# Attention on TensorE: from single heads in high and low parts to pairs of native float32 heads on the halves of the array

## The chip, the cores and the metric

One core of a Trainium2 chip runs one launch. The metric is the device time of the launch in microseconds. The kernel before takes 884.78 us (median of 3 runs, 884.65 to 886.75).

## What is computed

Attention with a causal window of 128 and a distance bias (batch 4, 8 heads, 576 positions, head dimension 64), then two feed-forward networks on the 2,304 x 512 result. From the reference:

```python
scores = scale * np.matmul(q, k.transpose(0, 1, 3, 2))
slopes = 2.0 ** (-8.0 * (np.arange(H, dtype=np.float32) + 1) / H)
bias = slopes[:, None, None] * (-np.abs(rel).astype(np.float32))[None, :, :]
mask = (rel >= 0) & (rel < window)
scores = np.where(mask, scores + bias[None], -1000000000.0)
...
attn = np.exp(scores)
attn = attn / (np.sum(attn, axis=-1, keepdims=True) + 1e-09)
return np.matmul(attn, v).astype(np.float32)
...
a = x @ w1
b = x @ w2
h = a * b @ w3
return (h @ w_out).astype(np.float32)
...
h = np.maximum(x @ w_in, 0.0)
return (h * h @ w_out).astype(np.float32)
```

The slope of head h is 2^-(h+1).

## The kernel before

**The whole.** The weights come as 64-bit words and are made into float32 on the chip (`conv_g`, `conv_s`, `conv_m`: two passes of VectorE over every weight tile on L307, two more on any engine). The product W3·W_out is formed first, native float32, on L733 (`p_w34`, 64 matmuls of 512 columns). Then, for each batch and each half of its 576 positions, `p_ab` multiplies x with W1 and W2 and `p_y` the product with W3·W_out; results go to DRAM as y. The second network follows with seven products in place of eight per 2x2 block (`p_r`, `p_o`). All large products but W3·W_out are float32 in two rounded parts: `mm3` (L165 to L168) sends high x high, high x low and low x high, one pass each.

**Attention.** A head has five blocks of 128 queries (the last one of 64 new queries), each against at most 256 keys. `p_qk` writes the scores of blocks 0 and 1, of 2 and 3 and of 4 into three PSUM tiles "s", of which there are two buffers, each one bank. `l_min` (L438, VectorE) adds the bias, reduces and stores the negated scores in "e" (block 4 in "p4"), `l_exp` (L446, ScalarE) takes the exponential, `l_sum` and `l_norm` divide. `p_tr1` and `p_tr2` transpose P on TensorE into PSUM tiles "t" (nine transposes of 128x128, L489 to L501; one uses a swapped identity, `swap`), `l_pth` copies them to SBUF, `p_pva` and `p_pvb` multiply with V, and `l_eva`, `l_evb`, `l_ad*` bring the result into `xf`. For each pair of heads `t_xh` and `t_xl` split `xf` into the high and low part of x, in tiles of half a batch's positions.

**Two kinds of head.** Heads 0 to 8 (`NQ`, `NV`, L16, L17) are native: q, k, V and P stay float32; the scores have 64 rows of contraction (`64*128` in the records), P·V has 64 output columns (`128*64`, its last piece `64*64`). k is first multiplied by 2^(h+1) (`t_kn`), so that one bias table `bm` serves all heads. TensorE records two matmuls and two weight loads for each native matmul. Heads 9 to 31 are split into high and low parts: q is stacked as high over low on 128 rows and met with k high and k low (L468, L469); V is laid side by side as high and low, and P high and P low are both sent through it (L528 to L532, L552), so that the partial results have to be added afterwards (L585, L590, L603).

**What sets the order.** `Plan` is given each step with a rank, engines and a cost, the steps it waits for and the buffers that it takes and gives back; `run()` then simulates the engines, picks among the steps that can start within 0.1 us the one of the lowest rank, and the instructions are recorded in that order for every engine. Heads have rank -13.66 + 10 n, the matmuls of the networks 1000 and more, so that heads go first where their data is ready. Each engine executes its own list in that order.

Of the kernel before, what the change touches and what calls it, by code (L numbers as in the profile page):

```python
# [15 lines left out]
NQ = frozenset(range(9))  # L16
NV = frozenset(range(9))  # L17
# [6 lines left out]
HALF = S // 2  # L24
WIN = 128


class Plan:
# [24 lines left out]
    def run(self):  # L53
# [15 lines left out]
        while ready:  # L69
            cands = []  # L70
            for n in ready:
# [3 lines left out]
                for h in takes:  # L75
                    p = pool[self.holds[h][0]]
                    if len(p) <= keep:
                        ok = False
                        break
                    t0 = max(t0, min(p))  # L80
# [44 lines left out]
def fused_kernel(  # L125
# [62 lines left out]
    swap = const.tile([128, 128], F32, name="swap")  # L188
    nc.gpsimd.memset(swap, 0.0)
    for base in (64, -64):  # L190
        nc.gpsimd.affine_select(
            out=swap, in_=swap, pattern=[[-1, 128]], compare_op=ALU.not_equal,
            fill=1.0, base=base, channel_multiplier=1,
        )
    bm = const.tile([128, 2 * WIN], F32, name="bm")
    nc.gpsimd.iota(
        bm, pattern=[[8, 2 * WIN]], base=-8 * WIN, channel_multiplier=-8,
# [3 lines left out]
        out=bm, in_=bm, pattern=[[-1, 2 * WIN]], compare_op=ALU.is_ge,  # L201
# [3 lines left out]
        out=bm, in_=bm, pattern=[[1, 2 * WIN]], compare_op=ALU.is_gt,  # L205
        fill=-1.0e30, base=0, channel_multiplier=-1,
    )

# [37 lines left out]
    def w_dma(kb, n=1):  # L246
# [4 lines left out]
            u=10, u34=4, wo=4, qkraw=1, qk=2, vraw0=1, vraw1=1, vs=2, e=2, p40=1, p41=1, s=2, t=1,  # L251
            pt1=1, pt2=1, a=1, b=1, xf=1, ta=1, tb=1, g=3, asb=2, gf=2, gt=8, ye=2,
            yA=14, yB=6, s0=1, t2a=1, t2b=1, v6=6, st=2, c1=2, U2=1, U4=1, U3=1, C=4, X=5, fo=4, fq=5, ww=4,
            **{f"x0_{k}": 1 for k in range(6)}, **{f"x1_{k}": 1 for k in range(8)},
# [82 lines left out]
    QS = [(i * 128, min(128, S - i * 128)) for i in range(5)]  # L337
    vraw = [at.tile([128, 5, D], F32, tag=f"vraw{i}", name=f"vraw{i}") for i in range(2)]
    for t in vraw:
        nc.gpsimd.memset(t[64:128, 4, :], 0.0)  # L340

    p4 = [at.tile([128, 256], F32, tag=f"p4{i}", name=f"p4{i}") for i in range(2)]
    for t in p4:
        nc.gpsimd.memset(t, 0.0)
    pts = {}


    def new_pt(nat):
        dt = F32 if nat else F32R
        t = at.tile([128, 1 if nat else 2, 1280], dt, tag="pt", name="pt")  # L350
        z = t[:, :, 512:768]
        nc.gpsimd.memset(z if dt == F32 else f(z), 0.0)
        pts[nat] = t

    HD = [dict() for _ in range(B * H)]
    xt = {}

    def t_load_qk(n):
        b, h = divmod(n, H)
        d = HD[n]  # L360
        if n in NQ:
            d["qs"] = at.tile([64, S], F32, tag="qs", bufs=2, name="qn")
            d["kh"] = at.tile([64, S], F32, tag="kh", bufs=2, name="kn")
            nc.sync.dma_start(out=d["qs"], in_=qk[b, h, 0])
            nc.sync.dma_start(out=d["kh"], in_=qk[b, h, 1])
        else:
            d["raw"] = at.tile([128, 2, S], F32, tag="qkraw", bufs=1, name="qkraw")
            for r in range(2):
                nc.sync.dma_start(out=d["raw"][64 * r:64 * r + 64], in_=qk[b, h].rearrange("t d s -> d t s"))

    def t_load_v(n):
        b, h = divmod(n, H)
        if n in NV:
            vd = HD[n]["vs"] = at.tile([128, 5, D], F32, tag="vs", bufs=2, name="vn")
        else:
            vd = vraw[n % 2]
        nc.sync.dma_start(out=vd[:, 0:4, :], in_=v_main[b, h].rearrange("p (c d) -> p c d", d=D))
        nc.sync.dma_start(out=vd[0:64, 4, :], in_=v_rest[b, h])

    def slope(n):  # L380
        return float(2 ** (n % H + 1))

    def t_kn(n, e):
        k = HD[n]["kh"]
        scaled(e, k, k, slope(n))

    def t_qh(n, e):
        d = HD[n]
        d["qs"] = at.tile([128, S], F32R, tag="qs", bufs=2, name="qs")
        copy(e, d["qs"], d["raw"][:, 0])  # L390

    def t_kh(n, e):
        d = HD[n]
        d["kh"] = at.tile([128, S], F32R, tag="kh", bufs=2, name="kh")
        nc.scalar.activation(out=d["kh"], in_=d["raw"][:, 1], func=ACTF.Copy, scale=slope(n))

    def t_ql(n, e):
        d = HD[n]
        sub(ENG[e], d["qs"][64:128], d["raw"][64:128, 0], f(d["qs"][64:128]))

    def t_kl(n, e):
        d = HD[n]
        d["kl"] = at.tile([128, S], F32R, tag="kl", bufs=2, name="kl")
        nc.vector.scalar_tensor_tensor(
            out=d["kl"], in0=d["raw"][:, 1], scalar=slope(n), in1=f(d["kh"]), op0=ALU.mult, op1=ALU.subtract
        )

    def t_vh(n, e):
        d = HD[n]
        vs = d["vs"] = at.tile([128, 5, 2 * D], F32R, tag="vs", bufs=2, name="vs")  # L410
        hi = (n % 2) * D
        copy(e, vs[:, :, hi:hi + D], vraw[n % 2])

    def t_vl(n, e):
        vs = HD[n]["vs"]
        hi = (n % 2) * D
        lo = D - hi
        sub(ENG[e], vs[:, :, lo:lo + D], vraw[n % 2], f(vs[:, :, hi:hi + D]))

    def part_of(n, i):  # L420
        if i == 4:
            return p4[n % 2][64:128, 0:192]
# [910 lines left out]
```

## Time and profile before

| | |
|---|---|
| time, median of 3 runs | 884.78 us |
| the single runs | 886.75, 884.65, 884.78 us |
| profiled execution, span from first to last instruction | 882.3 us |
| median of the runs less that span | 2.5 us |
| TensorE busy, matmuls | 868.4 us |
| VectorE, ScalarE, GpSimd busy | 680.2, 520.9, 191.9 us |
| HBM read, written | 90.67, 36.70 MB |

For the profiled execution the span alone is given; the fourth line shows what lies around it against the median run. Busy time of a matmul contains its tail in the array, so the length of a block of matmuls is read from start to start. In the rows, PE is TensorE's matmuls, PEld its weight loads, DVE VectorE, ACT ScalarE, POOL GpSimd; `64*128` means rows and columns of the array in use.

### The profile page before, as it was taken

To read this page: it belongs to the slowest core of one execution; us is meant where nothing else is said; L and a number is where in the kernel's file an instruction comes from. 1 tells how busy PE (TensorE), PEld (TensorE's weight loads), DVE (VectorE), ACT (ScalarE), POOL (GpSimd) and SP (SyncE) were. 2 spreads that over 40 slices of the span, in tenths; PEclk is the share of its full clock that TensorE was granted. 3 is DMA by queue.
4 is the path that set the end of the run, shared out by engine and by line. 5 is a ranking of instruction groups with operands and counts; after the bars stand their busy time and mean duration, and the time that the engine had idled before them with its cause. 6 is when DMAs were issued, how large, how long until landed. Compare 5 with 4: busy or idle time off the path is not lost.

```text
span 882.3 us, 16171 instructions
## 1 busy us (share of the span) xinstructions
PE 868.4 (98%) x5888; PEld 805.9 (91%) x5888; DVE 680.2 (77%) x1372; ACT 520.9 (59%) x1062; POOL 191.9 (22%) x234
## 2 busy tenths in 40 slices
PE   7999999999999999999999999999999899999998
PEld 4544459999999999999999999999999899999998
DVE  4878878888798897878676858775678888888772
ACT  5778766666767666667423446543566676556540
POOL 4212113222302312211010337351156200000000
PEclk7999999999999999999999999999999899999999
DMA  6787222441435334342477145453476564444310
GB/s 210 289 289 231 104 81 82 136 146 48 137 84 167 106 106 129 106 131 71 143 245 258 56 166 181 168 180 108 153 245 208 153 182 124 143 139 136 99 53 30
DMA packets 90703, 128.42 MB, mean 146 GB/s; under 512 B 8832, under 2 KB 70784, under 8 KB 88576
## 3 DMA queue, kind: packets, MB, share of 16 engines
q1 hardware_dynamic: 90624, 127.40, 45.7%
q8 instruction: 46, 0.75, 0.4%
q14 instruction: 33, 0.27, 0.1%
HBM read 90.67 MB, written 36.70 MB: 144 GB/s over the span
## 4 chain that ended last, share of the span: by engine, by line
PE 95%; DVE 2%; DMA 1%; issue 1%; ACT 1%; POOL 0%; SPq 0%; DVEq 0%; ACTq 0%; POOLq 0%
PE X L168 13%; PE X L166 13%; PE X L167 13%; PE g L166 11%; PE g L167 11%; PE g L168 11%; PE g L733 7%; PE s L466 2%; PE a L523 2%; PE t L489 2%; PE s L469 2%; PE s L468 1%; PE a L532 1%; PE b L552 1%; DMA m_scro<-u 1%; PE a L528 1%
## 5 line engine op out<-in xcount | busy, mean ns | idle before, releaser
L166 PE MATMUL g<-x,wu 128*128 128x288 f32 x512 | 154.1, 301 | 1.6 <-ACT a_sb L171 1.0
L167 PE MATMUL g<-x,wu 128*128 128x288 f32 x512 | 151.7, 296 | 0.0
L168 PE MATMUL g<-x,wu 128*128 128x288 f32 x512 | 151.1, 295 | 0.0
L166 PEld LDWEIGHTS g<-x,wu 128*128 128x128 f32 x512 | 96.4, 188 | 2.4 <-ACT a_sb L171 1.3
L167 PEld LDWEIGHTS g<-x,wu 128*128 128x128 f32 x512 | 96.8, 189 | 0.3 <-issue 0.3
L168 PEld LDWEIGHTS g<-x,wu 128*128 128x128 f32 x512 | 96.5, 188 | 0.0
L1119 ACT ACTIVATE C<-C 128x384 f32<-128x384 f32 x96 | 47.8, 521 | 64.8 <-issue 35.2
L166 PE MATMUL g<-gt,wu 128*128 128x288 f32 x256 | 76.5, 299 | 0.0
L167 PE MATMUL g<-gt,wu 128*128 128x288 f32 x256 | 75.7, 296 | 0.0
L168 PE MATMUL g<-gt,wu 128*128 128x288 f32 x256 | 75.4, 295 | 0.0
L213 POOL TENSOR_SCALAR e<-e,st 128x256 f32<-128x256 f32 (+1 forms) x59 | 29.3, 507 | 200.9 <-DVE st L456 136.8
L1093 DVE TENSOR_TENSOR C<-X,U 128x384 f32<-128x384 f32 (+1 forms) x99 | 51.2, 520 | 24.3 <-PE X L168 21.1
L446 ACT ACTIVATE e<-e,st 128x256 f32<-128x256 f32 (+1 forms) x128 | 60.5, 474 | 14.8 <-DVE st L438 14.2
L167 PE MATMUL X<-yA,u 128*128 128x384 f32 x192 | 65.0, 339 | 0.0
L166 PE MATMUL X<-yA,u 128*128 128x384 f32 x192 | 65.0, 339 | 0.0
L168 PE MATMUL X<-yA,u 128*128 128x384 f32 x192 | 65.0, 339 | 0.0
L733 PE MATMUL g<-raw 128*128 128x512 f32 x128 | 63.4, 625 | 0.0
L171 ACT ACTIVATE ww<-fq 128x1024 fp32r<-128x1024 f32 x35 | 37.0, 1059 | 42.4 <-PE X L168 24.1
L171 ACT ACTIVATE pt<-t 128x512 fp32r<-128x512 f32 (+1 forms) x64 | 38.3, 598 | 34.5 <-PE t L501 17.8
L167 PE MATMUL X<-u,ww 128*128 128x256 f32 x198 | 55.6, 281 | 0.0
L166 PE MATMUL X<-u,ww 128*128 128x256 f32 x198 | 55.5, 280 | 0.0
L168 PE MATMUL X<-u,ww 128*128 128x256 f32 x198 | 55.5, 280 | 0.0
(218 smaller groups left out, 2649.1 us busy)
## 6 DMA issues: line engine op xcount, KB each, us to landing
s_scr<-C SPq DMA_DIRECT2D x96, 192.0 KB, 2.0
u<-in_w2io_dram SPq DMA_DIRECT2D x32, 512.0 KB, 4.5
qkraw<-in_qk_dram SPq DMA_DIRECT2D x46, 288.0 KB, 4.2
fo<-s_scr SPq DMA_DIRECT2D x20, 512.0 KB, 4.1
raw<-in_w3t_dram SPq DMA_DIRECT2D x8, 1024.0 KB, 6.6
raw<-in_w_dram SPq DMA_DIRECT2D x8, 1024.0 KB, 6.1
fq<-s_scr SPq DMA_DIRECT2D x16, 512.0 KB, 4.1
y_scr<-ye SPq DMA_DIRECT2D x32, 144.0 KB, 1.8
```

The costliest lines, as they stand in the source:

```text
L166: nc.tensor.matmul(o, wh, xh, start=start, stop=False)
L167: nc.tensor.matmul(o, wh, xl, start=False, stop=False)
L168: nc.tensor.matmul(o, wl, xh, start=False, stop=stop)
L171: nc.scalar.activation(out=o, in_=i, func=ACTF.Copy)
L213: nc.gpsimd.tensor_scalar(out=o, in0=i, scalar1=c, scalar2=1.0, op0=ALU.mult, op1=ALU.mult)
L446: nc.scalar.activation(out=e, in_=e, func=ACTF.Exp, bias=st[:, 0, i:i + 1], scale=-1.0, accum_out=st[:, 1, i:i + 1],)
L466: nc.tensor.matmul(o, qb, d["kh"][:, k0:k1], start=True, stop=True)
L469: nc.tensor.matmul(o, qb, d["kl"][:, k0:k1], start=False, stop=True)
L489: nc.tensor.transpose(t[:, 128 * c:128 * c + 128], src, ident)
L733: nc.tensor.matmul(gw[fi], wl, wr, start=c == 0, stop=c == 7)
L1093: nc.vector.tensor_tensor(out=t_(o, tag), in0=bank[g, P], in1=cs[g, i], op=ALU.add)
L1119: nc.scalar.activation(out=x, in_=x, func=ACTF.Relu)
```

## The change

Two neighbouring heads are handled as a pair, all 32 heads native. q and k of the pair lie in one tile, the first head on partitions 0 to 63, the second on 64 to 127, and `p_qk` sends a matmul of the first head and one of the second in turn; each head writes its own score tile, so that a group of scores takes both buffers of "s". `p_pv` does the same with P·V: the first head fills PSUM partitions 0 to 63, the second 64 to 127 of one bank. `bm` is now a table per head, made by seven scalings of the first; k is no longer multiplied. All transposes use the plain identity. x is split straight from PSUM (`t_xh`, `t_xl`), into tiles of a whole batch's positions for which there are seven slots (`NX`), where there were six and eight of half the length. The planner now counts how many buffers of a kind a step takes. Ranks: -13.66 + 20 m for pair m; the other ranks stay.

```diff
+NE = 3
+NX = 7
...
+    bm = at.tile([128, H, 2 * WIN], F32, name="bm")
+    b0 = bm[:, 0]
     nc.gpsimd.iota(
...
+    for h in range(1, H):
+        nc.vector.tensor_scalar(out=bm[:, h], in0=b0, scalar1=0.5 ** h, scalar2=None, op0=ALU.mult)
...
+        if n % 2 == 0:
+            PR[n // 2]["qk"] = at.tile([128, 2, S], F32, tag="qk", bufs=2, name="qk")
+        r = 64 * (n % 2)
+        nc.sync.dma_start(out=PR[n // 2]["qk"][r:r + 64], in_=qk[b, h].rearrange("t d s -> d t s"))
...
         nc.vector.tensor_tensor_reduce(
             out=part_of(n, i), in0=ps, in1=bmi, op0=ALU.add, op1=ALU.min,
+            scale=-0.125, scalar=3.0e38, accum_out=stat[n % 4][rows(i), 0, i:i + 1],
         )
...
+    def p_qk(m, g):
+        t = PR[m]["qk"]
+        for r in range(2):
+            HD[2 * m + r].setdefault("s", []).append(ps_s.tile([128, 512], F32, tag="s", name="s"))
+        for i in ((0, 1), (2, 3), (4,))[g]:
+            q0 = min(128 * i, S - 128)
+            k0 = max(0, (i - 1) * 128)
+            w = min(S, (i + 1) * 128) - k0
+            o = 256 * (i % 2)
+            for r in range(2):
+                h = slice(64 * r, 64 * r + 64)
+                nc.tensor.matmul(
+                    HD[2 * m + r]["s"][g][:, o:o + w], t[h, 0, q0:q0 + 128], t[h, 1, k0:k0 + w],
+                    start=True, stop=True,
+                )
+
...
+    def l_pt(n, g, e):
+        if g == 0:
+            HD[n]["pt"] = at.tile([128, 1024], F32, tag="pt", bufs=NE, name="pt")
+        copy(e, HD[n]["pt"][:, 512 * g:512 * g + 512], HD[n]["t", g])
+
+    PV = (
+        ((0, 0, 0, 256), (1, 128, 256, 256), (2, 256, 512, 128)),
+        ((3, 0, 768, 192), (2, 0, 640, 128), (4, 128, 960, 64)),
+    )
+
+    def p_pv(m, g):
+        o = PR[m][g] = ps_v.tile([128, 512], F32, tag="ab"[g], name="ab"[g])
+        for x, (kb, c, src, w) in enumerate(PV[g]):
+            for r in range(2):
...
+                    o[64 * r:64 * r + 64, c:c + w], vt[m % 2][:, r, kb, :], HD[2 * m + r]["pt"][:, src:src + w],
+                    start=x == 0, stop=x == 2, skip_group_check=True,
...
+    def x_slot(m):
+        return m % NX
+
+    def t_xh(m, g, e):
+        b, p = divmod(m, H // 2)
+        if g == 0:
+            k = x_slot(m)
+            xt[b, p] = (xg if k < 4 else xb[0]).tile([128, 2, S], F32R, tag=f"x_{k}", name="x")
+        c0, c1 = XC[g]
+        copy(e, xt[b, p][:, 0, c0:c1], PR[m][g][:, 0:c1 - c0])
+
+    def t_xl(m, g):
+        b, p = divmod(m, H // 2)
+        c0, c1 = XC[g]
+        sub(nc.vector, xt[b, p][:, 1, c0:c1], PR[m][g][:, 0:c1 - c0], f(xt[b, p][:, 0, c0:c1]))
...
+        for g, w in enumerate((448, 512, 192)):
+            add(f"qk{g}_{m}", r + 1, {"pe": w_nat(w) + 0.1}, lambda e, g=g: p_qk(m, g), [f"ldq{n}" for n in heads] + last,
+                [f"s{g}_{n}" for n in heads], [f"qk{m}"])
+            last = [f"qk{g}_{m}"]
...
+        for g, w in enumerate((640, 384)):
+            add(f"pv{g}_{m}", r + 8, {"pe": w_nat(w) + 0.1}, lambda e, g=g: p_pv(m, g),
+                [f"pt{x}_{n}" for x in range(2) for n in heads] + [f"ldv{m}"], [f"{'ab'[g]}{m}"],
+                [f"v{m}"] + [f"pt_{n}" for n in heads])
+        k = x_slot(m)
+        hold(f"x{b}{p}", f"x_{k}", 4 * NF1)
+        for g, w in enumerate((QA, S - QA)):
+            add(f"xh{g}_{m}", r + 9, w_copy(w, True), lambda e, g=g: t_xh(m, g, e),
+                [f"pv{g}_{m}"] + ([f"xh0_{m}"] if g else ["gp"] if k >= 4 else []), [] if g else [f"x{b}{p}"], [f"{'ab'[g]}{m}"])
+            add(f"xl{g}_{m}", r + 9, w_tt(w, "d"), lambda e, g=g: t_xl(m, g), [f"xh{g}_{m}"], [], [f"{'ab'[g]}{m}"])
...
+    for m in range(B * H // 2):
+        add_pair(m, RANK["h0"] + 20.0 * m)
```

In the order of instructions this shows on TensorE. The names: s, t, a, b and g are PSUM tiles (scores, transposes, P·V, products), kh, kl, qs, qk, kn, qn hold q and k, pt is P transposed, v and vs are V, x and wu operands of the first network. First the stretch with the products of the first network, between two of its chains, before:

```order
L168 MATMUL g<-x_886,wu 128x288
L528 MATMUL a<-pt,vs 128x512
L529 MATMUL a<-pt,vs 128x256
L532 MATMUL a<-pt,vs 128x256 x4
L552 MATMUL b<-pt,vs 128x192 x4
L468 MATMUL s<-kh,qs 128x192
L469 MATMUL s<-kl,qs 128x192
L166 MATMUL g<-x_340,wu 128x288
```

and now, between two such chains:

```order
L169 MATMUL g<-x,wu 128x288
L448 MATMUL a<-pt,v_127 64x256 x4
L448 MATMUL a<-pt,v_127 64x128 x2
L448 MATMUL b<-pt,v_127 64x192 x2
L448 MATMUL b<-pt,v_127 64x128 x2
L448 MATMUL b<-pt,v_127 64x64 x2
L167 MATMUL g<-x,wu 128x288
```

P·V of one head, ten single-pass matmuls on the whole array and followed at once by the next head's scores, has become twelve native matmuls that go in turn to the first and the second head of a pair; the scores stand elsewhere, group by group. Second, the beginning, where W3·W_out (g<-raw) is formed, before:

```order
L466 MATMUL s<-kn,qn 128x192
L523 MATMUL a<-pt,vn 64x512
L523 MATMUL a<-pt,vn 64x256 x2
L545 MATMUL b<-pt,vn 64x192
L546 MATMUL b<-pt,vn 64x64
L466 MATMUL s<-kn,qn 128x192
L466 MATMUL s<-kn,qn 128x256 x3
L733 MATMUL g<-raw 128x512 x2
```

and now:

```order
L542 MATMUL g<-raw 128x512
L416 MATMUL s<-qk 128x256 x4
L448 MATMUL a<-pt,v_127 64x256 x4
L448 MATMUL a<-pt,v_127 64x128 x2
L448 MATMUL b<-pt,v_127 64x192 x2
L448 MATMUL b<-pt,v_127 64x128 x2
L448 MATMUL b<-pt,v_127 64x64 x2
L542 MATMUL g<-raw 128x512 x3
L416 MATMUL s<-qk 128x192 x2
L416 MATMUL s<-qk 128x128 x2
L416 MATMUL s<-qk 128x256 x2
```

Where P·V and scores of one head stood together, a group of scores of a later pair, P·V of a whole pair and pieces of W3·W_out now follow each other. Counted over the whole list, TensorE has 44 separate blocks of scores (`L416`) and 16 of P·V (`L448`) with 51 returns to matmuls of the whole array; before there were 16 blocks of native scores, 9 of native P·V and 21 returns. Up to the last matmul of W3·W_out the new list has the scores of five pairs and P·V of four, the old one all of heads 0 to 8 and the scores of head 9.

## Rows read from the trace of the kernel before

**Rows 1.** The page, busy time of each engine, its share of the span, instructions.

```profile
PE 868.4 (98%) x5888; PEld 805.9 (91%) x5888; DVE 680.2 (77%) x1372; ACT 520.9 (59%) x1062; POOL 191.9 (22%) x234
```

**Rows 2.** Stretches: busy us of PE, PEld, DVE, ACT, POOL; clock; DMA share; GB/s.

```profile
20.00:128.00 108.00, 107.31 (x365) 53.93 (x364) 88.39 (x189) 81.63 (x173) 20.86 (x27) 1.00 0.59 203
128.00:440.00 312.00, 311.38 (x2404) 309.36 (x2403) 257.96 (x692) 205.13 (x524) 67.96 (x92) 1.00 0.39 112
```

**Rows 3.** The page, the chain that ended last, by engine.

```profile
PE 95%; DVE 2%; DMA 1%; issue 1%; ACT 1%; POOL 0%; SPq 0%; DVEq 0%; ACTq 0%; POOLq 0%
```

**Rows 4.** Waits of TensorE: who, for whom, us in total, times, longest.

```profile
PE t L622 <- POOL bm L204: 3.4, 1, 3.4
PE X L168 <- DVE st L174: 2.2, 1, 2.2
```

**Rows 5.** Timeline of TensorE, native heads: start, us, instruction, shapes, count.

```profile
23.60 0.33 PE L497 MATMUL t<-swap,p 128*128 128x128 f32 x1
23.77 0.27 PE L498 MATMUL t<-ident,p 128*128 128x128 f32 x1
...
23.98 0.27 PE L500 MATMUL t<-ident,e 128*128 128x128 f32 x1
24.09 0.27 PE L501 MATMUL t<-ident,e 128*128 128x128 f32 x1
24.30 0.59 PE L466 MATMUL s<-kn,qn 64*128 64x192 f32 x2
24.81 1.94 PE L523 MATMUL a<-pt,vn 128*64 128x512 f32 x6
26.59 0.49 PE L545 MATMUL b<-pt,vn 128*64 128x192 f32 x2
27.00 0.33 PE L546 MATMUL b<-pt,vn 64*64 64x64 f32 x2
27.26 1.89 PE L466 MATMUL s<-kn,qn 64*128 64x192 f32 x8
29.07 2.08 PE L733 MATMUL g<-raw 128*128 128x512 f32 x4
31.08 0.59 PE L466 MATMUL s<-kn,qn 64*128 64x192 f32 x2
31.60 0.66 PE L489 MATMUL t<-ident,e 128*128 128x128 f32 x4
```

**Rows 6.** The same for a head in high and low parts.

```profile
181.34 0.25 PE L468 MATMUL s<-kh,qs 128*128 128x192 f32 x1
...
182.28 0.29 PE L166 MATMUL g<-x,wu 128*128 128x288 f32 x1
...
185.95 0.33 PE L468 MATMUL s<-kh,qs 128*128 128x192 f32 x1
...
186.24 0.32 PE L166 MATMUL g<-x,wu 128*128 128x288 f32 x1
...
189.46 0.40 PE L528 MATMUL a<-pt,vs 128*128 128x512 f32 x1
...
190.72 0.60 PE L489 MATMUL t<-ident,e 128*128 128x128 f32 x4
```

**Rows 7.** Groups by line and shape: busy us, mean ns of one, idle before.

```profile
L733 PE MATMUL g<-raw 128*128 128x512 f32 x128 | 63.4, 625 | 0.0
...
L307 DVE SCALAR_TENSOR_TENSOR raw<-raw 128x1024 uint32<-128x1024 uint32 x40 | 50.0, 1257 | 3.9 <-issue 1.8 <-POOL p L213 1.3
...
L438 DVE CUSTOM_DVE_ANT_0 e<-s,bm 128x256 f32<-128x256 f32 x96 | 37.1, 418 | 0.6 <-PE s L469 0.4
...
L174 DVE TENSOR_TENSOR pt<-t,pt 128x512 fp32r<-128x512 f32 x46 | 31.6, 688 | 5.7 <-ACT pt L171 4.5
...
L404 DVE SCALAR_TENSOR_TENSOR kl<-qkraw,kh 128x576 fp32r<-128x576 f32 x23 | 19.0, 824 | 1.9 <-ACT kh L395 1.7
...
L603 DVE TENSOR_TENSOR xf<-a,ta 64x512 f32<-64x512 f32 x23 | 15.8, 686 | 0.9 <-POOL ta L590 0.4
```

More of the change, by code (lines that the diff above doesn't have):

```diff
@@ L186, in fused_kernel @@
     make_identity(nc, ident)
[L188 to L195, printed above, removed]
+    bm = at.tile([128, H, 2 * WIN], F32, name="bm")
+    b0 = bm[:, 0]
     nc.gpsimd.iota(
-        bm, pattern=[[8, 2 * WIN]], base=-8 * WIN, channel_multiplier=-8,
+        b0, pattern=[[4, 2 * WIN]], base=-4 * WIN, channel_multiplier=-4,
         allow_small_or_imprecise_dtypes=True,
@@ L334, in add_weights @@
         add("cl" + k, rank, w_tt(1024), lambda e: conv_lo(key, e), ["ch" + k], [], ["raw" + k])
[L337 to L342, printed above, removed]
+    QA = 384
+    vt = [at.tile([128, 2, 5, D], F32, tag=f"v{i}", name=f"v{i}") for i in range(2)]
+    for t in vt:
+        nc.gpsimd.memset(t[64:128, :, 4, :], 0.0)
+    p4 = [at.tile([128, 256], F32, tag=f"p4{i}", name=f"p4{i}") for i in range(4)]
     for t in p4:
         nc.gpsimd.memset(t, 0.0)
[L345 to L353, printed above, removed]
+    stat = [at.tile([128, 3, 5], F32, tag=f"st{i}", name=f"st{i}") for i in range(4)]
+    for t in stat:
+        nc.gpsimd.memset(t, 1.0)
     HD = [dict() for _ in range(B * H)]
+    PR = [dict() for _ in range(B * H // 2)]
     xt = {}
@@ L359, in t_load_qk @@
         b, h = divmod(n, H)
[L360 to L385, printed above, removed]
@@ L444, in l_exp @@
         e = part_of(n, i)
-        st = HD[n]["st"][128 - QS[i][1]:128]
+        st = stat[n % 4][rows(i)]
         nc.scalar.activation(
@@ new lines, in p_tr @@
+    def p_tr(n, g):
+        e, q = HD[n]["e"], p4[n % 4]
+        t = HD[n]["t", g] = ps_t.tile([128, 512], F32, tag="t", name="t")
+        if g == 0:
+            todo = ((0, e[:, 0, 128:256]), (128, e[:, 1, 0:128]), (256, e[:, 1, 128:256]), (384, e[:, 2, 0:128]))
+        else:
+            todo = (
+                (384, q[:, 128:256]), (320, q[:, 0:128]), (256, e[:, 3, 128:256]),
+                (0, e[:, 2, 128:256]), (128, e[:, 3, 0:128]),
+            )
+        for c, src in todo:
+            nc.tensor.transpose(t[:, c:c + 128], src, ident)
@@ L537, in p_pvb @@
-    def p_pvb(n):
-        d = HD[n]
-        vs = d["vs"]
-        pt = pts[n in NV]
-        o = ps_v.tile([128, 512], F32, tag="b", name="b")
-        d["b"] = o
-        if n in NV:
-            o = o[(n % 2) * 64:(n % 2) * 64 + 64]
-            nc.tensor.matmul(o[:, 0:192], vs[:, 3, :], pt[:, 0, 1088:1280], start=True, stop=False)
-            nc.tensor.matmul(
-                o[:, 128:192], vs[0:64, 4, :], pt[0:64, 0, 768:832], start=False, stop=True
-            )
-            return
-        for kb, c in ((3, 1088), (4, 640)):
-            for part in range(2):
-                nc.tensor.matmul(
-                    o[:, 0:192], vs[:, kb, :], pt[:, part, c:c + 192],
-                    start=(kb == 3 and part == 0), stop=(kb == 4 and part == 1),
-                )
```

337 lines of the change are left out of this document (71 added, 266 removed).

## The prediction

> **What bounds the kernel now.** I read the busy shares first: TensorE is busy for 98% of the span, VectorE for 77%, ScalarE for 59% [rows 1]. The table by stages shows three stretches of interest: a start of 20 us, then 20 to 128 us (the products W3·W_out and the first nine heads), then 128 to 440 us (the other 23 heads between the products of the first network). In the second TensorE is busy for 107.31 of 108 us, in the third for 311.38 of 312 [rows 2], always at the full clock. The chain that ended last is TensorE for 95% of its length [rows 3], and the waits of TensorE that the trace can name are one of 3.4 us at the start and some of 2.2 us and less [rows 4]. So the time is the length of TensorE's own stream: what VectorE, ScalarE and the DMA queues are spared is worth nothing by itself, and each column that TensorE streams, each weight load that stands open and each pause between matmuls counts.
>
> What the attention costs on TensorE is read from the starts of its blocks. A native head (0 to 8): the eight records of its first four score blocks (960 columns, two passes each) run from 27.26 to 29.07 us, the last block (192 columns) from 31.08 to 31.60, P·V from 24.81 to 27.26 [rows 5]: 1.81 + 0.52 + 2.45 = 4.78 us. A head in high and low parts (9 to 31): scores 181.34 to 182.28 and 185.95 to 186.24, P·V 189.46 to 190.72 [rows 6]: 0.94 + 0.29 + 1.26 = 2.49 us. The two score blocks of the native head differ by 768 columns and 1.29 us: **1.68 ns for a column of a native matmul**, 0.84 ns in each pass. What is left of the 0.52 us after 192 columns is 0.20 us, which does not grow with the columns: the first weights are loaded in the open, and the array empties before it changes its division. The same shows elsewhere: the last transpose before a block of halves takes 0.21 us from start to start (24.09 to 24.30) where its neighbour takes 0.11, and the first one behind such a block 0.17 (23.60 to 23.77) [rows 5]. So a full-array stretch between two blocks pays 0.16 us. P·V pays 0.06 at its start (1.78 us for 1,024 columns, that is 1.72) and 0.09 behind its 192 columns (0.41 for 0.32): 0.15.
>
> Before, then: 9 x 4.78 + 23 x 2.49 + 21 returns to the full array x 0.16 = 43.0 + 57.3 + 3.4 = **103.7 us**.
>
> **The change on TensorE.** A head now has 1,088 score columns (128 + 3 x 256 + 192) and 1,024 in P·V, all native: 2,112 x 1.68 = 3.55 us. All 32 heads: 113.5 us if the two halves of the array take turns. The order shows 44 blocks of scores and 16 of P·V with 51 returns to the full array, as each group of scores needs both score banks and so stands alone between other work: 44 x 0.20 + 16 x 0.15 + 51 x 0.16 = 19.4 us. The trace before never has two matmuls on different halves next to each other, so the overlap of the halves is not shown and is bounded. Upper end, no overlap: 113.5 + 19.4 = 132.9, **29.2 us more**. Lower end, full overlap: 56.8 + 19.4 = 76.2, 27.5 us less.
>
> I take a value between, from the order of the passes. A matmul is two passes, and the program gives first head, second head, first head and so on. A pass must follow the pass before it on its own half and cannot start ahead of the pass before it in the stream. So the second pass of the first head runs beside the first pass of the second, and the next pair joins on; only the first and the last pass of a block are alone. Two matmuls of 256 columns on each half take 5 x 0.215 = 1.08 us where eight passes in turn take 1.72; the group of 128 and 256 also 1.08, since a pass of 128 columns (0.107) is no longer than the load of its weights (0.20 less the 0.09 of the emptying, 0.11); the group of 192 takes 3 x 0.161 = 0.49; P·V, with six matmuls a half, 2.00 instead of 3.44. Together 4.65 us a pair, 16 x 4.65 + 19.4 = 93.8, **9.9 us less** than before. I choose this over no overlap because of the row nearest to it: the array pauses when the division changes, even between two P·V matmuls of one head (26.59 to 27.00, from 128*64 to 64*64), and not between matmuls of one division [rows 5]; the hardware does hold the halves as units. If the halves' weight loads run beside each other too, the group of 128 and 256 columns takes 0.86 instead of 1.08, 3.5 us less in all; that is the low end of the forecast. The Trainium skill, "TensorEngine Tiling (Array Packing)", Key Properties, says that different tiles load weights and multiply in parallel; by that rule the sum would be 13.4 us less than before, and no run here shows it.
>
> **How much of it arrives.** Of the 103.7 us, 47.6 lie ahead of 128 us: the nine native heads with their returns and the scores of the tenth head. The new order has there, up to the last product of W3·W_out, the scores of five pairs and P·V of four: 5 x 2.65 + 4 x 2.00 + 11 blocks x 0.20 + 4 x 0.15 + 14 returns x 0.16 = 26.3 us, so TensorE has 21 us less to do. From 128 us on it has 11 more: a pair costs 5.9 us with its pauses, two heads in parts 4.98. In the earlier stretch VectorE is busy for 88.39 of 108 us [rows 2], of it 40 passes of 1,257 ns over the weight words [rows 7], which stay as they are. VectorE's list up to the last weights for W3·W_out, at the durations of the trace, adds up to 83 us, about 5 less than before. From 128 to 440 us VectorE is busy for 257.96 of 312 us, 0.83 [rows 2]. At that share 83 us take 100, while TensorE would be through after 87. So between 0 and 13 us of the 21 do not come; I take 4, as TensorE can draw heads forward.
>
> Nothing else is on the path. VectorE loses the low parts of P (46 x 688 ns), of K (23 x 824), the sums into x (23 x 686), 66 us in all [rows 7], and shorter pieces beside them. The third stretch is covered by TensorE, which stands idle there for 0.62 us by the records [rows 2]; so this is worth 0, and I allow 3 us for waits too short to show as idle. The seven new table scalings, 256 columns each, are put at no more than a reduction of 256 columns (0.42 us [rows 7]), 3 us at the start, under the first scores; the table is built without the swap matrix ahead of it, which can only shorten the 3.4 us [rows 4]. The late heads' q and k were loaded twice each and are now loaded once, covered. The new wait, scores of a group until VectorE has read both banks (four reductions of 0.42 us [rows 7], 1.7 us), has behind it on TensorE the products of the network, which the order puts in between: 24 of them between the last two groups of a pair; eight shorter ones take 0.94 us [rows 6], so these take 2.8 us or more. A pair that waits for its slot of x has the second products of the batch as cover.
>
> Sum: 882.3 - 9.9 + 4 = 876.4 us of span. The median of the runs shown is 884.78, 2.5 above the span of the profiled execution: **878.9 us**.
>
> **The rivals.**
> 1. The halves do not overlap, and the change doesn't do what it says: 884.8 + 29.2 = 914. For it: no record before shows overlap, and native matmuls run pass after pass. Against it: the pauses at each new division. It decides as soon as a second head's first pass starts after the end of the first head's second. This is the other side.
> 2. Weights are loaded ahead by one matmul alone, so the second half's first pass starts 0.11 us (scores) or 0.06 us (P·V) behind the pass beside it, and the next ones slip: scores 3.18 a pair instead of 2.65, P·V 2.38 instead of 2.00; 16 x 0.9 = 14 more, 893. For it: no row shows a load that runs ahead of two matmuls, and 0.20 us stand open at every block. With P·V alone so, 16 x 0.38 = 6 more: 885. For that form speaks the Trainium skill, "TensorE: Matmul & The Clock Gate", What overlaps and what doesn't: weight loads overlap running matmuls only when their row groups differ; the two halves of P·V share their rows. No row here decides it.
> 3. The stretch up to 128 us is handed to VectorE and the weight words: 13 to all of the 21 us do not come, 884.8 - 9.9 + 17 = 892. For it: the share of 0.83, and ScalarE at 81.63 of 108 us [rows 2]. Against it: W3·W_out is 63.4 us of TensorE [rows 7] and stands between the heads in small pieces. It decides when the last weights for W3·W_out are ready later than about 112 us.
>
> **How the numbers follow.** Forecast 0.50 (its own range 868 to 888: with parallel loads and nothing lost 871, with 13 lost 888, and 3 beyond the low end for VectorE's relief), no overlap 0.25, loads one ahead in both 0.07, in P·V alone 0.08, VectorE as the bound 0.10. A difference of 0.3%, 2.7 us, is about what a measurement of this kernel can tell. Faster: 0.42 of the forecast and 0.01 of the rest, 0.43. Same: 0.05 of the forecast, 0.05 of P·V alone, 0.02 of the third, 0.12. Slower: 0.03 + 0.25 + 0.07 + 0.02 + 0.08 = 0.45. The range 868 to 915 takes in the case of no overlap and the low end.
>
> **What would show it.** In the trace after: a group of scores with 256 columns takes about 1.1 us plus 0.2 from start to the next work, not 1.7 plus 0.2; P·V about 2.15 us, not 3.6. W3·W_out ends some 16 us sooner than at 128 us. From there to the end of the attention TensorE stays above 99%, with about 0.9 us more for a pair than two heads had. Scores of 1.9 us a group would make the prediction wrong by the first rival; a TensorE that stands idle before 110 us, by the third.

## The result, and the profile after the change

The changed kernel takes **864.76 us** (median of four runs, 864.54 to 865.28), the kernel before 884.71 beside it (884.32 to 886.75): a ratio of 0.977, 95% interval 0.9758 to 0.9782. The forecast was 878.9 with a range from 868 to 915. The direction was right, the size was not: the change brings 20 us, more than three times the 5.9 foreseen, and the time lies below the range. The profiled execution took 865.28 us, its span is 863.4.

TensorE is still the bound. The page's line that answers to [rows 1]:

```profile
PE 846.0 (98%) x5952; PEld 774.7 (90%) x5952; DVE 565.3 (65%) x1146; ACT 449.2 (52%) x932; POOL 159.3 (18%) x199
```

The stretches that answer to [rows 2] (busy us of PE, PEld, DVE, ACT, POOL; granted clock; DMA share; GB/s):

```profile
20.00:128.00 108.00, 104.13 (x495) 58.84 (x494) 88.43 (x180) 74.36 (x165) 27.19 (x31) 0.96 0.58 194
128.00:440.00 312.00, 312.00 (x2460) 291.95 (x2461) 177.26 (x508) 158.34 (x435) 42.25 (x66) 1.00 0.40 127
```

Two things are new. VectorE falls from 0.83 to 0.57 of the third stretch. And TensorE, which had 0.69 us without work between 20 and 128 us, now has 3.87, at a mean clock of 0.96.

Where the time comes from is seen in single blocks. The timeline of TensorE for a group of scores with 256 columns, two matmuls of each head (start, us from the first start to the last end, instruction, count):

```profile
200.45 0.60 PE L432 MATMUL t<-ident,e 128*128 128x128 f32 x4
200.98 1.13 PE L416 MATMUL s<-qk 64*128 64x256 f32 x8
202.04 0.40 PE L167 MATMUL g<-x,wu 128*128 128x288 f32 x1
```

The next work starts 1.06 us after the group. That is 0.86 us for eight passes, and the 0.20 us that [rows 5] gave for a block's open load and emptying; the forecast said 1.08 and 0.20. The same view cut to the first hundredth of a microsecond of this block, and the instructions of the line there (durations in ns, smallest, median, largest):

```profile
200.98 0.49 PE L416 MATMUL s<-qk 64*128 64x256 f32 x2
```

```profile
L416 PEld LDWEIGHTS s<-qk x2: 182/182/183, 201.0 to 201.0; 64*128 64x128 f32 x2
L416 PE MATMUL s<-qk x2: 480/480/480, 201.0 to 201.0; 64*128 64x256 f32 x2
```

Two passes and two weight loads are under way at once: each pass is recorded with 0.48 us, and both lie within 0.49. By the single records the first pass of the second head starts 6 ns after the first pass of the first head, and so on for all four pairs of passes, 0.215 us apart. The second head does not wait for the first head's second pass. P·V, and the score group with 128 columns behind it:

```profile
209.88 1.30 PE L448 MATMUL a<-pt,v 128*64 128x256 f32 x12
211.02 0.83 PE L448 MATMUL b<-pt,v 128*64 128x192 f32 x12
211.77 0.93 PE L416 MATMUL s<-qk 64*128 64x128 f32 x8
212.63 0.40 PE L167 MATMUL g<-gt,wu 128*128 128x288 f32 x1
```

P·V of a pair takes 1.89 us (forecast 2.15 with its pauses), the group of 128 and 256 columns 0.86 (forecast 1.28 with them).

TensorE's time, counted from the start of one pass to the start of the next, with idle time apart; the warm-up matmuls at the very start, 3.6 us before and 3.7 after, are left out:

| us | before | after | difference |
|---|---|---|---|
| scores | 51.4 | 44.5 | -6.9 |
| P·V | 52.5 | 30.6 | -21.9 |
| transposes, with the returns to the full array | 30.3 | 32.8 | +2.5 |
| W3·W_out | 59.8 | 60.7 | +0.9 |
| all other products, with returns | 670.5 | 673.6 | +3.0 |
| idle | 7.6 | 11.2 | +3.6 |

The last product of W3·W_out in the timelines (start, us), before and after:

```profile
128.22 0.61 PE L733 MATMUL g<-raw 128*128 128x512 f32 x1
```

```profile
111.42 0.61 PE L542 MATMUL g<-raw 128*128 128x512 f32 x1
```

It ends at 112.0 us (before: 128.8), 16.8 sooner. From there to TensorE's last product it is 747.9 us, 2.5 less than before. The added idle time is in the first 112 us (7.8 us, in the kernel before 2.0 up to the same product); the waits of TensorE there (who, for whom, us in total, times, longest), which answer to [rows 4]:

```profile
PE t L432 <- ACT pt L172: 3.9, 5, 0.8
PE t L474 <- POOL bm L199: 2.7, 1, 2.7
PE s L416 <- DMA qk<-in_qk_dram: 1.9, 2, 1.2
PE s L416 <- DVE st L383: 1.8, 3, 0.9
PE g L542 <- DVE raw L303: 0.3, 1, 0.3
```

The second of these is the wait ahead of TensorE's first matmul, which the 7.8 us do not count.

### The profile page after: what moved, and what is told of

The parts are those of the page before. It is cut to its first block, busy times and chain, and to the rows that moved or that the text cites. A ratio compares the mean times of both kernels' runs of the same rounds, so it can differ in the third digit from the quotient of the medians.

```text
span 863.4 us, 15706 instructions
## 1 busy us (share of the span) xinstructions
PE 846.0 (98%) x5952; PEld 774.7 (90%) x5952; DVE 565.3 (65%) x1146; ACT 449.2 (52%) x932; POOL 159.3 (18%) x199
## 4 chain that ended last, share of the span: by engine, by line
PE 96%; DVE 1%; DMA 1%; SPq 0%; ACT 0%; issue 0%; DVEq 0%
PE X L169 14%; PE X L168 14%; PE X L167 14%; PE g L167 13%; PE g L169 12%; PE g L168 12%; PE g L542 7%; PE s L416 4%; PE t L432 4%; PE a L448 2%; PE b L448 1%; DMA qk<-in_qk_dram 1%; ACT pt L172 0%; DVE fq L980 0%; SPq L353 0%
## 5 line engine op out<-in xcount | busy, mean ns | idle before, releaser
L595 DVE TENSOR_TENSOR gf<-g,a_sb 128x288 f32<-128x288 f32 x64 | 29.2, 457 | 103.3 <-PE g L169 100.3
L172 ACT ACTIVATE a_sb<-g 128x288 f32<-128x288 f32 x64 | 26.2, 410 | 92.0 <-PE g L169 91.9
L902 DVE TENSOR_TENSOR C<-X,U 128x384 f32<-128x384 f32 (+1 forms) x99 | 51.1, 520 | 26.7 <-PE X L169 21.0
L383 DVE CUSTOM_DVE_ANT_0 e<-s,bm 128x256 f32<-128x256 f32 (+1 forms) x128 | 43.8, 386 | 32.2 <-PE t L432 15.7
L210 POOL TENSOR_SCALAR e<-e,st 128x256 f32<-128x256 f32 (+1 forms) x58 | 29.3, 519 | 152.3 <-DVE st L399 83.8
L167 PE MATMUL X<-u,ww 128*128 128x256 f32 x198 | 55.5, 280 | 0.0
```

What stands on the lines that cost most here:

```text
L167: nc.tensor.matmul(o, wh, xh, start=start, stop=False)
L172: nc.scalar.activation(out=o, in_=i, func=ACTF.Copy)
L210: nc.gpsimd.tensor_scalar(out=o, in0=i, scalar1=c, scalar2=1.0, op0=ALU.mult, op1=ALU.mult)
L383: nc.vector.tensor_tensor_reduce(out=part_of(n, i), in0=ps, in1=bmi, op0=ALU.add, op1=ALU.min, scale=-0.125, scalar=3.0e38, accum_out=stat ...
L902: nc.vector.tensor_tensor(out=t_(o, tag), in0=bank[g, P], in1=cs[g, i], op=ALU.add)
```

## The experiments

Two questions: do the halves really run beside each other, and what sets how far one may run ahead? And what took back some 9 us of a gain that, with full overlap, would have been 27.5? The theory drawn from the trace: each half works through a list of its own; and in the start the gain meets waits and half clock. The rivals stand in each expectation.

**Both heads' scores on one half.** In the scores of the odd heads

```
-                h = slice(64 * r, 64 * r + 64)
+                h = slice(0, 64)
```

> The second head's scores are computed on the first head's half of the array, so the two heads' score matmuls must take turns; P·V stays as it is (the odd heads get the scores of the even ones: that part of the computation is changed). Theory 1 (the gain comes from the two halves running side by side): a pair's scores cost 2 x 1.83 instead of 1.83 us, 16 x 1.83 = 29 us more than the changed kernel, of which the idle time of the first 105 us may take back up to 7: 887 to 894 us. Theory 2 (the gain comes from the low parts that are gone, and the halves' overlap is small): at most 5 us more, below 870. In the trace under theory 1 the second head's first pass starts a whole matmul behind the first head's, under theory 2 as in the changed kernel.

Measured: 897.09 us, ratio to before 1.0135 (1.0112 to 1.0157). The scores take 72.2 us of TensorE, 27.6 more than in the repeat of the changed kernel told of below; 29.3 were expected. The group that took 1.06 us:

```profile
199.90 1.99 PE L416 MATMUL s<-qk 64*128 64x256 f32 x8
201.82 0.44 PE L432 MATMUL t<-ident,p 128*128 128x128 f32 x2
```

1.92 us, or 1.72 for eight passes in turn. Theory 1 holds: with the same instructions in the same order, the scores' gain hangs on the second half alone. One point of the expectation falls: the idle time of the start took nothing back (TensorE is idle for 12.9 us, in the changed kernel for 11.2), and the time lies 3 us above the range.

**The second head behind the first.** The loops over heads and blocks change places, in scores and in P·V:

```
-        for x, (kb, c, src, w) in enumerate(PV[g]):
-            for r in range(2):
+        for r in range(2):
+            for x, (kb, c, src, w) in enumerate(PV[g]):
...
```

> Inside each block of scores and of P·V all matmuls of the first head are issued, then all of the second; nothing else differs. Theory 1 (each half of the array works through its own list, and a list may run several matmuls ahead of the other): the two heads still overlap, 864 to 867 us, and the second head's first pass of a P·V block starts within 0.1 us of the first head's. Theory 2 (a half is only started while the matmul beside it in the program is still running, so neighbours alone can overlap): only the last matmul of the first head runs beside the first of the second; P·V of a pair 3.2 instead of 1.9 us and scores 2.9 instead of 1.8, 16 x 2.4 = 38 us more, less some idle time: 893 to 903 us.

Measured: 873.37 us, 0.9867 (0.9845 to 0.9889), between the two. The scores lose nothing (43.2 us in all), P·V 7.7 us (38.0 in place of 30.2). A block of P·V:

```profile
213.31 1.35 PE L448 MATMUL a<-pt,v 128*64 128x256 f32 x9
...
214.88 0.88 PE L448 MATMUL b<-pt,v 128*64 128x128 f32 x9
215.68 0.50 PE L416 MATMUL s<-qk 64*128 64x128 f32 x4
```

2.37 us to the next work in place of 1.89. The same timeline cut to the block's first 0.01 us, and to the instant 213.80:

```profile
213.31 0.43 PE L448 MATMUL a<-pt,v 128*64 128x256 f32 x1
```

```profile
213.58 0.65 PE L448 MATMUL a<-pt,v 128*64 128x256 f32 x3
```

At the start one half works alone, where two did before. At 213.80 the second head's first pass has joined: it starts 6 ns after the first pass of the first head's second matmul, and 0.43 us ahead of the first head's third matmul (214.23), which comes earlier in the program. In the scores, with two matmuls a head in a block, the second head starts 13 to 14 ns behind the first. Both theories fall in part; the reading that fits is that a half holds one matmul that runs and one that waits, and that a third one holds up everything behind it in the program.

There is a rival: TensorE as a whole takes three matmuls and no fourth, which would give the same starts. The weight loads speak against it. At 214.07 us two are under way:

```profile
214.01 0.19 PEld L448 LDWEIGHTS a<-pt,v 128*64 128x64 f32 x2
```

By their order one is for the first head's third matmul (214.01), the other for the second head's second (214.07). The second matmul of the first head and the first of the second still run then, so four are taken. If four fitted whatever their half, the second head could have started with the block.

**Two of one head, then two of the other.** A test of that reading: in each group of P·V the first two matmuls of the first head, the first two of the second, then the third of each.

```
-        for x, (kb, c, src, w) in enumerate(PV[g]):
-            for r in range(2):
+        for xs in ((0, 1), (2,)):
+            for r, x in ((r, x) for r in range(2) for x in xs):
```

> In each group of P·V the first two matmuls of the first head, then the first two of the second, then the third of each; nothing else differs. Theory 1 (drawn from the run with the heads one after the other, where the second head's first matmul started 6 ns behind the first head's second: a half holds one matmul that runs and one that waits, and a third holds up all behind it): two of a head fit, the second head starts within 0.02 us of the first, P·V of a pair takes 1.9 us as in the changed kernel, 863.5 to 866.5 us. Theory 2 (each change between a head's own matmuls and the other head's costs time, or the list is shorter than two): P·V of a pair 2.1 to 2.3 us, 868 to 872 us.

Measured: 867.39 us (866.31 to 869.25), 0.9797 (0.9774 to 0.9821). A block of P·V:

```profile
211.23 1.31 PE L449 MATMUL a<-pt,v 128*64 128x256 f32 x12
212.36 0.88 PE L449 MATMUL b<-pt,v 128*64 128x192 f32 x12
213.17 0.71 PE L416 MATMUL s<-qk 64*128 64x128 f32 x6
```

Theory 1 holds in the trace: the second head's first pass starts 14 ns behind the first's, and a block goes from 211.23 to 213.17, 1.94 us, 0.05 more than in the changed kernel. P·V takes 31.1 us in all (30.2 to 30.6 without the edit). The 0.05 us fit the reading too: at the start of the second group two matmuls of the first head follow its third of the first group, again three in a row, and the second head's first pass there takes 0.21 us to the next one, the first head's 0.16. The time is above what was expected, and not for P·V's sake alone: in the profiled execution TensorE is idle for 12.5 us, with a wait of 2.4 us at 12.6 us for the second pair's q and k.

**All heads native, but single.** In the kernel before:

```
-NQ = frozenset(range(9))
-NV = frozenset(range(9))
+NQ = frozenset(range(32))
+NV = frozenset(range(32))
```

> The kernel before with all 32 heads native and single: no low parts, no pairs. Theory 1 (pairs side by side are the whole gain, and the relief of VectorE is worth nothing): 23 heads cost 4.78 instead of 2.49 us, 53 us more than before, and up to 4 us for returns to the full array: 934 to 942 us. Theory 2 (a part of the gain comes from the work that VectorE and ScalarE no longer have): below 930 us.

Measured: 944.57 us, 1.0671 (1.0648 to 1.0695): 60 us slower than before. Scores and P·V grow by 54.1 us (52.7 expected), the transposes with their returns by 6.0, 2 more than allowed for, so that the time lies 2.6 us above the range of theory 1. VectorE's relief (599.7 us busy, before 680.2) shows nowhere. So of the two things that the change does to the attention, native arithmetic costs 60 us, and the pairs on halves, with what else comes with them, give back 80.

**Spare matmuls in the start.** Full-array matmuls of 256 columns, whose results nothing reads, where TensorE was idle between 7 and 24 us:

```
+        for _ in range(n):
+            nc.tensor.matmul(fill[0][:, 0:256], ident, bm[:, 0], start=True, stop=True)
...
+                if m == 1 and g == 0 and r == 0 and i == 0:
+                    p_fill(2)
+        if m == 0:
+            p_fill(3)
...
+        if n < 4:
+            p_fill(2)
```

> The changed kernel with 29 spare full-array matmuls of 256 columns (their results are not used) put into TensorE's idle time between 7 and 24 us. Theory 1 (the idle gaps there let the clock fall to half, and the half clock up to 28 us costs the changed kernel 2 to 3 us more than the kernel before): the granted clock rises ahead of 24 us, W3·W_out ends 2 to 5 us sooner than at 111.4 us, 860 to 863 us. Theory 2 (VectorE, ScalarE and the loads set the start, so a faster TensorE only waits longer): W3·W_out ends within 1 us of 111.4, 864 to 867 us.

Measured: 868.27 us, 0.9805 (0.9784 to 0.9825). They were 27, and 8 of them stood behind the second pair's transposes, at 36 to 45 us, where they cost what the others had won: W3·W_out ends at 112.2 us, the changed kernel's 112.0 (the 111.4 of the expectation is the start of that last product). Behind it this execution takes 3.3 us longer than the changed kernel's, 1.3 of them idle; the cause of that stays open. A second run has n < 2 in the last condition (19 spare matmuls, all ahead of 24 us):

> As the run with spare matmuls, but those between transposes stand only behind the first pair's transposes (19 matmuls, all ahead of 24 us); in that run 8 of 27 stood behind the second pair's, at 36 to 45 us, and TensorE, 2.4 us ahead at 28.4 us, was 0.2 us behind at 45. Theory 1 (the half clock up to 28 us costs the changed kernel about 2.4 us): TensorE is 2.4 us ahead at 28.4 us and W3·W_out ends 1.5 to 2.5 us sooner than at 112.0 us, 861.5 to 863.5 us. Theory 2 (VectorE, ScalarE and the loads hand out the first stretch): the lead is gone by 112 us, 864 to 866 us.

Measured: 865.16 us (863.12 to 868.07), 0.9779 (0.9744 to 0.9815). The stretch from 24 to 28 us, of the changed kernel:

```profile
24.00:28.00 4.00, 4.00 (x12) 1.58 (x13) 3.33 (x3) 2.11 (x4) 1.85 (x1) 0.50 0.98 315
```

and with the spare matmuls:

```profile
24.00:28.00 4.00, 4.00 (x36) 2.56 (x35) 3.95 (x8) 2.31 (x8) 1.59 (x1) 1.00 1.01 325
```

The kernel before, whose clock was at half from 12 to 20 us, is at full clock there:

```profile
24.00:28.00 4.00, 4.00 (x20) 2.33 (x19) 3.23 (x10) 3.49 (x12) 0.64 (x1) 1.00 0.97 387
```

In the profiled execution with spare matmuls TensorE is 2.5 us ahead at 28.4 us, keeps all of it to the end of W3·W_out (109.6 us), and gives back 0.8 in one wait at 202 us. So between these two executions half clock in the start makes about 2.4 us, nearly all of it behind 23 us, where TensorE has work. It is not the same in every execution: in the repeat of the changed kernel told of below, without spare matmuls, passes run at full rate again from 25.5 us on, W3·W_out ends at 110.7 us, and the span is 861.8 us, as here (861.7). Against that one the spare matmuls bring 1.1 us at the end of W3·W_out. In the median nothing can be told: the executions differ by 5 us among themselves.

**The changed kernel again, and the second pair's q and k loaded earlier,** without and with the 19 spare matmuls:

```
-            add(f"ldq{n}", r, {"dma": w_dma(295)}, ...
+            add(f"ldq{n}", -12.0 if m == 1 else r, {"dma": w_dma(295)}, ...
```

> The changed kernel itself once more, as the yardstick for the two runs beside it. All theories: 864 to 868 us; where an execution is slower than 865, the second pair's q and k land later than at 13.9 us and its first scores wait for them.

> The changed kernel with the loads of the second pair's q and k ahead of the first two loads of weight words on the queue of SyncE (they stand behind 2 MB of words, and TensorE waited for them until 13.95 us in the changed kernel, until 17.80 us in the run with half the word passes); the planner works out its order anew. Theory 1 (a pair needs two heads' q and k at once, and their place in the queue is a part of what the start loses, and of the spread between executions): the wait for q and k is gone, W3·W_out ends 1 to 3 us sooner than in the changed kernel beside it, 861 to 864 us, spread over executions below 2 us. Theory 2 (the words that land 1.5 us later hold W3·W_out up by as much): within 1 us of the changed kernel.

> The early loads of the second pair's q and k together with the 19 spare matmuls of the second run with them. Theory 1 (idle wait and half clock add up): 1.5 to 2.5 us less than with the early loads alone, 859 to 862 us. Theory 2 (once the loads are early, TensorE has little idle time there, and the clock rises by itself): within 1 us of the early loads alone.

Measured: 865.13 us for the changed kernel (863.58 to 866.34), 870.22 (870.03 to 871.88) and 870.18 (868.95 to 872.34) for the others. W3·W_out ends at 110.7, 110.2 and 108.9 us. With the early loads TensorE waits for no q and k any more in the first 112 us, and the spread is small; but the planner's new order pays 3.5 us of new waits after 112 us, the longest 2.6 us at 257 us for ScalarE's copy of a transposed group, and 2.0 more in the products. Theory 1 is right on the wait and wrong on the time; W3·W_out ends 0.5 us sooner, not 1 to 3, as TensorE's other waits ahead of that end grow (9.0 us idle in all, in the repeat 6.7). The 19 spare matmuls bring the end of W3·W_out forward by 1.3 us more and nothing to the time, so that theory 2 of that run holds by its time. What the repeat's expectation says of executions over 865 us can't be seen, as the profiled one is the fastest. What the place of the loads alone is worth stays open, since the planner changed the order everywhere.

**Half of VectorE's passes over the words of W3 and W_out.**

```
-        low, high = raws[key][:, :, 0], raws[key][:, :, 1]
+        n = 1024 if key[0] == "w12" else 512
+        low, high = raws[key][:, :n, 0], raws[key][:, :n, 1]
```

> VectorE's two bit-mask passes over each tile of words of W3 and W_out go over 512 instead of 1,024 columns (24 passes about 0.6 us shorter, 14 us of VectorE ahead of 112 us; the other half of these words keeps wrong bits, so that part of the computation is changed). The order is the same on every engine. Theory 1 (VectorE hands out the first stretch: the bits of the weight words, together with the reductions of the pairs): TensorE's idle time and half clock ahead of 112 us shrink, W3·W_out ends 4 to 8 us sooner, 856 to 861 us. Theory 2 (the loads, and the chain from the first scores over ScalarE's copies to the first P·V, hand it out, whatever VectorE has to do): W3·W_out ends at most 2 us sooner, 862 to 865 us.

Measured: 865.53 us (863.77 and 867.29), 0.9774 (0.9737 to 0.9811). VectorE is busy for 69.8 of the first 112 us, in the changed kernel for 85.0, and neither execution is faster than those of the changed kernel (863.58 to 866.34 in its repeat). TensorE's waits ahead of 40 us, in its profiled execution, the slower one:

```profile
PE s L417 <- DMA qk<-in_qk_dram: 6.7, 2, 6.3
PE t L475 <- POOL bm L199: 2.7, 1, 2.7
PE t L433 <- ACT pt L172: 2.2, 3, 0.8
PE s L417 <- DVE st L384: 1.8, 3, 0.9
```

The wait for the second pair's q and k is 6.3 us long here. The waits for ScalarE's copies and for free score banks are what they were in the changed kernel (2.2 and 1.8 us). W3·W_out ends at 114.3 us, 2.3 later than there, with 4.8 us more of the wait for q and k. So theory 1 falls by the time of both executions, 863.77 and 867.29 us: VectorE's words do not hand out the first stretch. The end of W3·W_out with the short wait was not seen.

**Other banks for the first pair's transposes,** with the planner's order anew (its list of buffers is changed to match), and then with the order of the changed kernel on every engine:

```
-        t = HD[n]["t", g] = ps_t.tile([128, 512], F32, tag="t", name="t")
+        t = HD[n]["t", g] = (ps_g if n < 2 else ps_t).tile([128, 512], F32, tag="g" if n < 2 else "t", name="t")
```

> The first pair's transposes go to PSUM banks of the W3·W_out products, which are free until 23 us, instead of the one bank for transposes, so that they need not wait for ScalarE's copy of the group before (three waits of 0.8, 0.7 and 0.8 us). The planner works out its order anew. Theory 1 (these waits and the half clock behind them are a part of what the start lost): the three waits are gone, W3·W_out ends 1.5 to 3 us sooner than at 112.0 us, 861 to 863.5 us. Theory 2 (what follows the transposes, ScalarE's copies and the words, sets the start): at most 1 us sooner, 864 to 866 us.

> The first pair's transposes go to banks of the W3·W_out products, as in the run with spare banks, but the order on every engine stays that of the changed kernel. Theory 1 (three waits of 0.8, 0.7 and 0.8 us for ScalarE's copies are TensorE time that the start lost): the waits between the four groups of transposes are gone, W3·W_out ends about 2 us sooner, 862 to 864 us. Theory 2 (the wait moves to what stands behind the transposes, the words of W3 and W_out and the second pair's scores): TensorE is idle by as much before 36 us, 864 to 866 us.

Measured: 867.35 us (865.06 to 871.90), 0.9786 (0.9755 to 0.9817), and 865.60 (863.33 to 865.94), 0.9771 (0.9752 to 0.979). In the first the profiled execution waited for q and k for 4.9 us, which hides the rest. For the second, the timeline of the changed kernel (in brackets the idle time before, and who ended it):

```profile
16.89 1.11 PE L432 MATMUL t<-ident,e 128*128 128x128 f32 x4
18.78 0.66 PE L432 MATMUL t<-ident,p 128*128 128x128 f32 x2 [0.78 <-ACT pt L172]
19.24 0.85 PE L432 MATMUL t<-ident,e 128*128 128x128 f32 x3
20.77 1.11 PE L432 MATMUL t<-ident,e 128*128 128x128 f32 x4 [0.69 <-ACT pt L172]
22.66 0.66 PE L432 MATMUL t<-ident,p 128*128 128x128 f32 x2 [0.78 <-ACT pt L172]
23.12 0.85 PE L432 MATMUL t<-ident,e 128*128 128x128 f32 x3
23.76 1.06 PE L542 MATMUL g<-raw 128*128 128x512 f32 x1
```

and with other banks:

```profile
16.64 1.11 PE L432 MATMUL t<-ident,e 128*128 128x128 f32 x4
17.54 0.63 PE L432 MATMUL t<-ident,p 128*128 128x128 f32 x2
17.97 1.59 PE L432 MATMUL t<-ident,e 128*128 128x128 f32 x7
19.40 0.38 PE L432 MATMUL t<-ident,p 128*128 128x128 f32 x2
19.61 0.49 PE L432 MATMUL t<-ident,e 128*128 128x128 f32 x3
22.43 0.93 PE L542 MATMUL g<-raw 128*128 128x512 f32 x1 [2.32 <-ACT pt L172]
```

Three waits of 2.25 us in sum have become one of 2.32, ahead of the first product of W3·W_out, whose bank still waits for one of the same copies. Theory 2 holds by the time and by TensorE's idle time before 36 us (7.6 us, in the changed kernel 6.2): the wait for ScalarE's copies moves. But the first product starts 1.3 us sooner here, and W3·W_out ends at 110.2 us, 1.8 sooner than at 112.0, which is theory 1's sign; against the repeat (110.7) it is 0.5. What the banks are worth by themselves is not told apart from what executions differ by. No version that was run beats the changed kernel by more than the runs of one kernel differ.

## Why the prediction was wrong

- **What bounds the kernel**: right. TensorE is busy for 98% before and after, and the 115 us that VectorE lost show nowhere; the run with all heads native and single shows it once more.
- **The price of a native column and of a pause**: right. 1.72 us for eight passes in turn, 0.86 for four pairs; 0.20 us for a score block, which the 33 blocks behind 112 us bear out (11 pairs, 26.9 us: 11 x 1.83 + 33 x 0.20 = 26.7).
- **The order of the passes**: this is the step that failed. "A pass must follow the pass before it on its own half and cannot start ahead of the pass before it in the stream" has a wrong second part. The second head's first pass starts 6 to 7 ns behind the first head's, ahead of that one's second pass: each half works through its own list, and both run their two passes in step. So a pair costs 3.55 us in columns, not 4.65: 16 x 1.10 = 17.6 us. The lower end of that term, 27.5 us less, was the right value. The forecast's argument for a value between was a guess on an order that no row showed. The Trainium skill, "TensorEngine Tiling (Array Packing)", Key Properties, says that different tiles load weights and multiply in parallel; here the trace agrees, with loads and passes 6 to 7 ns apart. The prediction cited it, took from it the loads alone (13.4 us less), and kept the chain of passes beside it; with the matmuls in parallel too, its sum is the lower end, 27.5 us less.
- **What does not arrive**: the 4 us were too small. With full overlap TensorE has 26.5 us less to do ahead of the end of W3·W_out (the forecast's 21.3 before rounding, 0.82 us more for the scores of each of five pairs and 0.28 for P·V of each of four), and that end came 16.8 us sooner: 9.7 us did not arrive. Of these 5.9 are idle time (7.8 us ahead of that end, before 2.0); 2.6 are scores and P·V, 22.8 us less where their prices give 25.4; 0.9 are W3·W_out and 0.8 transposes with their returns; 0.5 come back, as TensorE starts sooner. The forecast has no term for the clock: with the 19 spare matmuls, at full clock, scores, transposes and W3·W_out take 7.1 us less than in the changed kernel, and with the spare matmuls' own time W3·W_out still ends 2.5 us sooner. The forecast looked at VectorE's share for this term; the waits are for the second pair's q and k, ScalarE's copies and score banks, in the first 64 us.
- **The two together**: 876.4 - 17.6 + 4.6 = 863.4 us of span, as measured. The 4.6 are 5.7 more lost in the start (9.7, not 4) and 0.4 more behind TensorE's last product, less 1.5, by which the stretch between is shorter than full overlap at the forecast's prices makes it (2.5 us, not 1.0).
- **The rivals**: no overlap (0.25) and loads one ahead (0.15 together) are excluded by the rows of the blocks. For the second, the Trainium skill, "TensorE: Matmul & The Clock Gate", What overlaps and what doesn't, says that weight loads overlap running matmuls only when their row groups differ; P·V's halves share their rows, and the trace shows no cost of it: 1.89 us a pair, the price of full overlap and one pause. The third rival, the first stretch handed out by others, is there in part, but with VectorE's passes over the words cut by half the time does not fall, so its mechanism was wrong.
- **The signs**: W3·W_out ends 16.8 us sooner, as forecast (16), but by luck, as two errors cancel: 5.2 us more gained, 5.7 more lost. Behind it TensorE stays above 99%, as said (busy for all of the 244 us from 112 to 356); the 0.9 us more for a pair is not there, that stretch is 2.5 us shorter.

The range missed because its lower end allowed for parallel loads (3.5 us) but not for parallel passes. The bound stood in the text, 17.6 us below the value chosen, with no chance given to it.

## What to carry to other kernels

Where no row shows whether two units overlap, both ends of the bound deserve a chance of their own, above all the simple one; a mechanism that lies between them is worth its own row first. Two float32 matmuls on halves of the array, issued in turn, cost one; alternate them in the program (two of one half in a row cost 0.05 us a pair here, three 0.48). In the start of this program a gain on the bounding engine was paid out only as fast as loads and copies came.

## What the runs showed of the hardware

- A half of the array that has one matmul running and one waiting takes no third, and the third holds up the other half's matmuls behind it (P·V of a pair 2.37 us in place of 1.89 with three in a row, 1.94 with two). Both halves together had four matmuls running or waiting. A later matmul of the program on the free half started 0.43 us ahead of an earlier one.
- The granted clock of a row does not show every fall. In the repeat of the changed kernel the stretch from 16 to 20 us has a clock of 1.00,

```profile
16.00:20.00 4.00, 3.19 (x13) 1.76 (x10) 1.84 (x5) 2.72 (x7) 2.44 (x4) 1.00 1.00 406
```

and yet the four transposes in its timeline take as long as those at 16.89 us of the changed kernel shown above, where the record has 0.50 (that is 1.2 GHz), and not 0.60 us as those at 200.45 us:

```profile
16.77 1.11 PE L432 MATMUL t<-ident,e 128*128 128x128 f32 x4
```

So the time from pass to pass is the safer reading.
- Executions of one kernel differ by up to 7 us here (the run with spare banks, 865.06 to 871.90), where those of the kernel before, on the same chips, differ by 4. In the three profiled executions where the wait for the second pair's q and k was longest (6.3, 4.9 and 2.4 us), the time was 867 to 872 us. But with other banks in the same order TensorE waited 2.6 us at the same place, by the profile for VectorE, and that execution took 863.33; that this load is the cause was not shown.
